# Convolution and two wide layers on one core: the two row halves of the array write the same PSUM banks by turns, without a swapped copy of x

## Chip, cores and metric

The kernel runs on one core of one Trainium2 chip, in one launch. The metric is the device time of the program in microseconds, lower is better.

## What is computed

The inputs are x (2 x 4096 tokens x 192) and weight_gen (2 x 4096 x 8 heads x 7 taps) in float32, and two pairs of weights (192 x 2048 and 2048 x 192) that arrive as float64. Cut to what matters:

```
w   = softmax(weight_gen over its 7 taps)
y   = causal convolution of x, 7 taps, one set per token and head (24 channels a head)
h1  = y @ w_in1;   y2  = max(0.01*h1, h1) @ w_out1        # layer 1
h2  = y2 @ w_in2;  out = max(h2, 0)**2 @ w_out2           # layer 2
```

## The kernel before

**Arithmetic.** TensorE works on fp32r. Every operand is split into a high part and a low remainder (xh, xl; gh, gl; wh, wl), and a product is the three terms hh, lh and hl. A float64 weight arrives as two 32-bit words; `piece` (lines 252 to 351) rebuilds a float32 from them and splits it.

**Blocks and steps.** The 8192 tokens are 16 blocks of 512. A layer takes 8 steps per block; a step makes 256 of the 2048 hidden channels with `mm1` (540 to 559) and, LAG = 2 steps later, multiplies them back to 192 with `mm2` (580 to 610). Each matmul uses 64 rows of the array: `HALVES[0]` or `HALVES[1]`, issued in pairs that run side by side. One step is 9 pairs of `mm1` and 10 of `mm2`. All matmuls of half 0 write other PSUM banks than those of half 1: in `mm1` bank d of `ph` belongs to half d, in `mm2` each half has its own accumulators pa and pb (four banks, one set, so a block's first `mm2` waits until the last block's sums are read). Because 192 input channels are 128 + 64, each half needs both halves of the first 128: `swap` (377 to 385) copies x's halves across by DMA, or `turn` (387 to 396) by TensorE for blocks 0 and 1.

**Other engines.** `activate` (561 to 578) reads `ph` twice on ScalarE in layer 1 (lines 568, 569) and takes three ScalarE operations in layer 2 (571 to 573); VectorE then makes gl (576). `local_sum` (413 to 533) computes softmax and convolution on VectorE: 7 products (473) and 6 sums (485); for block 1 five of the sums, and for most first-layer weights one sum (`plus`, 245), go through GpSimd as adding DMAs. Blocks 0 and 1 are transposed by TensorE (498), the later ones by VectorE and a trip through DRAM. `end1`/`again` (627 to 656) park layer 1's result in DRAM and bring it back; `end2` (658 to 677) adds the halves' sums, moves 64 rows by DMA, transposes and stores.

**Order.** `Plan.op` records each operation with a priority, `Plan.issue` (68 to 138) fixes the order of every engine's queue ahead of the run: an engine takes the first operation in order of priority that can start, TensorE always in strict order. The order of blocks is layer 1 of blocks 0 to 4, then layer 2 of block 0, layer 1 of block 5, layer 2 of block 1, and so on; block 1 begins at step 8.

Of the kernel before, what the change touches and what calls it, by code (L numbers as in the profile page):

```python
# [13 lines left out]
SIGN_EXP = -(1 << 23)  # L14
# [127 lines left out]
def kernel(  # L142
# [40 lines left out]
    EARLY = 2  # L183
    R = TB * H
# [19 lines left out]
    MM = 0.2345  # L204
# [14 lines left out]
    def weight_tiles(pool, l):  # L219
        wi.append({k: pool.tile([P, 3, NPR, P], F32R, name=f"wi{l}{k}") for k in "hl"})  # L220
        wo.append(pool.tile([P, NFC, 2 * D], F32R, name=f"wo{l}"))

    warm = const.tile([P, 1], F32, name="warm")
# [4 lines left out]

# [16 lines left out]
    def plus(to, tv, of, ov, pr, late):  # L245

        pl.op(
            "POOL", 1.0, pr, [of, to], [to],
            lambda: nc.gpsimd.dma_start(out=tv(), in_=ov(), accum_op=ALU.add), late=late,
        )  # L250

    def piece(kind, l, j, nj, pr, dma=False, gate=()):
# [11 lines left out]
        if kind == "i":  # L264
            src = (w_in1, w_in2)[l].rearrange("(s p) (n e m) w -> p s n e (m w)", p=Q, e=2, m=P)
            for d in range(2):

                def load(d=d):
                    to = raw.t[HALVES[d], :n, :].rearrange("p (s q m) w -> p s q (m w)", s=3, m=P)
                    for q in range(nj):  # L270
                        nc.sync.dma_start(out=to[:, :, q], in_=src[:, :, j + q, d])

                pl.op("SP", 0.5 * nj, pr - 6, [], [raw], load, late=(nj * 0.6, 3.5), after=gate[:1])
# [13 lines left out]
        def I(b):  # L287
            return b.t[:, :n].bitcast(I32)

        pl.op(  # L290
            "ACT", act(n), pr - 3, [raw], [wu, wa],
# [16 lines left out]
            "DVE", dve2(n), pr - 2, [wa], [wu],  # L308
            lambda: nc.vector.tensor_scalar(I(wu), I(wa), SIGN_EXP, None, op0=ALU.bitwise_and),  # L309
        )  # L310
        pl.op(
            "DVE", dve(n), pr - 2, [wu, raw], [wu],
            lambda: nc.vector.scalar_tensor_tensor(  # L313
                V(wu), raw.t[:, :n, 0].bitcast(U32), 2.0**-52, V(wu), op0=ALU.mult, op1=ALU.mult
            ),
        )
        if dma:
            plus(wa, lambda: V(wa), wu, lambda: V(wu), pr - 2, (nj * 0.8, 4.5))
        else:
            pl.op(  # L320
                "DVE", dve(n), pr - 2, [wu, wa], [wa],
                lambda: nc.vector.tensor_tensor(V(wa), V(wa), V(wu), op=ALU.add),
            )
        def to(hl):
            if kind == "i":
                return wi[l][hl][:, :, js, :].rearrange("p s q m -> p s (q m)")
            return wo[l][:, 2 * j : 2 * (j + nj), slice(0, D) if hl == "h" else slice(D, 2 * D)]

        def val():
            return V(wa).rearrange("p (s m) -> p s m", s=3 if kind == "i" else 2 * nj)  # L330
# [23 lines left out]
    xrows = x.rearrange("b s d -> (b s) d")  # L354
# [13 lines left out]
    XS = ("ah", "al", "sh", "sl", "bh", "bl")  # L368
# [4 lines left out]

    sets = {}
    taken = []

    def swap(xs, pr):
        for k in "hl":

            def go(k=k):  # L380
                to, of = xs["s" + k].t, xs["a" + k].t
                nc.sync.dma_start(out=to[0:Q].bitcast(F32), in_=of[Q:P].bitcast(F32))
                nc.sync.dma_start(out=to[Q:P].bitcast(F32), in_=of[0:Q].bitcast(F32))

            pl.op("SP", 1.0, pr, [xs["a" + k]], [xs["s" + k]], go, late=(0.8, 2.0))

    def turn(xs, pe, pr):

        pt = pl.buf(ps, [P, 2, N], F32, "pt", "ph", 2)
        for i, k in enumerate("hl"):  # L390
            pl.op(
                "PE", MM, pe + 0.1 * i, [xs["a" + k], perm_b], [pt],
                lambda i=i, k=k: nc.tensor.matmul(pt.t[:, i, :], lhsT=perm, rhs=xs["a" + k].t, start=True, stop=True),
            )
        for i, k in enumerate("hl"):
            pl.op("ACT", act(N), pr, [pt], [xs["s" + k]], lambda i=i, k=k: nc.scalar.copy(xs["s" + k].t, pt.t[:, i, :]))
# [16 lines left out]
    def local_sum(tb, pr, gate=()):  # L413
# [53 lines left out]

# [8 lines left out]
        for k in range(1, K):  # L476
            tmp = pl.buf(sb, [P, TB, H, G], F32, "tmp", "c", 2)
            pl.op("DVE", dve(TB * D), pr - 2, [xc, wg], [tmp], lambda k=k, tmp=tmp: prod(k, tmp.t))
            if tb == 1 and k < K - 1:
                flat = lambda: att.t[:, :, 0:D]  # L480
                plus(att, flat, tmp, lambda tmp=tmp: tmp.t.rearrange("p t h g -> p t (h g)"), pr - 2, (1.6, 4.5))
            else:
                pl.op(
                    "DVE", dve(TB * D), pr - 2, [att, tmp], [att],
                    lambda tmp=tmp: nc.vector.tensor_tensor(acc(), acc(), tmp.t, op=ALU.add),  # L485
                )
# [43 lines left out]
        if tb < EARLY:  # L530
            turn(xs, at[0, tb] - 0.3, pr - 1)
        else:
            swap(xs, pr - 1)

# [5 lines left out]
    def mm1(l, tb, j, pr):  # L540
        xs = sets[l, tb]
        ph = h_t[l, tb, j] = pl.buf(ps, [P, 2, N], F32, "ph", "ph", 2)

        def go():
            wh, wl = wi[l]["h"], wi[l]["l"]

            terms = [(w, hl, s) for ss in ("ab", "s") for w, hl in ((wh, "h"), (wl, "h"), (wh, "l")) for s in ss]
            for i, (w, hl, s) in enumerate(terms):
                for d in range(2):
                    c = 2 if s == "b" else d ^ (s == "s")  # L550
                    nc.tensor.matmul(  # L551
                        ph.t[:, d, :],
                        lhsT=w[HALVES[d], c, j, :],
                        rhs=xs[s + hl].t[HALVES[d]],
                        start=(i == 0),
                        stop=(i == len(terms) - 1),
                    )

        return pl.op("PE", 9 * MM, pr, [*xs.values(), wi_b[l][j]], [ph], go)
# [20 lines left out]
    def mm2(l, tb, j, pr):  # L580
        gh, gl = g_t.pop((l, tb, j))
        first, last = j == 0, j == NPR - 1
        if first:
            acc_t[l] = [
                [pl.buf(ps, [P, N], F32, n, f"q{2 * d + i}", 1) for i, n in enumerate(("pa", "pb"))] for d in range(2)
            ]
        acc = acc_t[l]

        def prods(terms, g, begin, end):
            for i, (c, w) in enumerate(terms):  # L590
                for d in range(2):
                    wt = wo[l][HALVES[d], 2 * j + c, :]
                    nc.tensor.matmul(  # L593
                        acc[d][w == "b"].t,
                        lhsT=wt[:, {"ah": slice(0, P), "b": slice(P, 2 * P), "al": slice(2 * P, 3 * P)}[w]],
                        rhs=g.t[HALVES[d], c, :],
                        start=begin and i == 0,
                        stop=end and i == len(terms) - 1,
                    )

        w = wo_b[l][j]
        for n, (ks, g) in enumerate(((("ah", "al"), gh), (("b",), gh), (("ah",), gl), (("b",), gl))):
            terms = [(c, k) for c in range(2) for k in ks]
            to = [a[ks[0] == "b"] for a in acc]
            pl.op(
                "PE", len(terms) * MM, pr + 0.01 * n, [g, w], to,
                lambda terms=terms, g=g, n=n: prods(terms, g, first and n < 2, last and n >= 2),
            )
        if last:
            (end1, end2)[l](tb, acc, pr - 1)  # L610


    def total(acc, i, v, hold, pr):
        o = pl.op("ACT", act(N), pr, [acc[1][i]], [v, *hold], lambda: nc.scalar.copy(v.t, acc[1][i].t))
        pl.op(
            "DVE", dve(N), pr, [acc[0][i], v], [v],
            lambda: nc.vector.tensor_tensor(v.t, acc[0][i].t, v.t, op=ALU.add),  # L617
        )
        return o

# [3 lines left out]

    kept = {}

    def end1(tb, acc, pr):
        kept[tb] = [pl.buf(dram, [P, N], F32, n, n, LEAD + 2) for n in ("ka", "kb")]
        for i in range(2):
            v, to = wide("s", ("e", 2)), kept[tb][i]  # L630
            total(acc, i, v, [], pr)
            pl.op("SP", 0.5, pr, [v], [to], lambda v=v, to=to: nc.sync.dma_start(out=to.t, in_=v.t), late=(0.8, 2.0))

    def again(tb, pr, gate):
# [9 lines left out]
        def twice():  # L644
            for v, rows in ((bu, slice(0, Q)), (bl_, slice(Q, P))):
                for d in range(2):
                    nc.sync.dma_start(out=v.t[HALVES[d]], in_=kb.t[rows])
# [121 lines left out]
```

## Time and profile before

| what | us |
|---|---|
| median of three runs | 1173.73 |
| lowest, highest run | 1172.78, 1175.06 |
| profiled execution, its span (first to last instruction) | 1175.6 |
| TensorE busy | 1125.3 (96%) |
| VectorE busy, ScalarE busy | 724.4 (62%), 748.6 (64%) |

The page has no time for the profiled execution besides its span. That lies 1.9 us above the median of the timed runs, so sums below are made against 1175.6 and their differences taken to the median. TensorE is the busy engine over most of the span; its busy time does not tell how fast it works, which has to be read from the distance of its matmuls.

### The profile page before, as it was taken

How to read it: one execution, taken by the hardware profiler on the slowest of the kernel's cores; microseconds unless marked ns; L12 is line 12 of the kernel's file. 1: busy time of each engine (PE TensorE's matmuls, PEld its weight loads, DVE VectorE, ACT ScalarE, POOL GpSimd, SP SyncE). 2: the span in 40 equal slices, each digit the busy share in tenths (PEclk: the TensorE clock that was granted, in tenths of full speed). 3: DMA queues.
4: the chain of work that ended last, by engine and by line, in shares of the span. 5: the costliest groups of instructions: out<-in, count | busy, mean ns of one | idle time of the engine just before them, and what ended most of it. 6: DMA issues, size and time to landing. Idle time of an engine off the chain costs nothing.

```text
span 1175.6 us, 22999 instructions
## 1 busy us (share of the span) xinstructions
PE 1125.3 (96%) x9748; PEld 926.9 (79%) x9748; DVE 724.4 (62%) x871; ACT 748.6 (64%) x830; POOL 15.8 (1%) x20
## 2 busy tenths in 40 slices
PE   2689999999999999999999999999999999999996
PEld 1469887888888888888888888888888888888885
DVE  7989999948556484755738475574846543344333
ACT  2545467585756748576574857657585665777774
POOL 0210000000000000000000000000000000000000
PEclk9989999999999999999999999999999999999999
DMA  8964646151421314142141513214151232121111
GB/s 183 224 108 106 143 119 169 32 146 23 120 50 60 92 41 128 19 116 53 45 107 33 136 19 100 65 34 122 27 143 19 90 80 50 48 64 37 19 20 18
DMA packets 112798, 94.29 MB, mean 80 GB/s; under 512 B 59644, under 2 KB 89114, under 8 KB 112696
## 3 DMA queue, kind: packets, MB, share of 16 engines
q1 hardware_dynamic: 108712, 87.99, 29.9%
q0 software_dynamic: 3792, 4.72, 2.5%
q8 instruction: 76, 1.25, 0.4%
q14 instruction: 26, 0.21, 0.1%
q10 hardware_dynamic: 192, 0.11, 0.0%
HBM read 50.06 MB, written 20.19 MB: 60 GB/s over the span
## 4 chain that ended last, share of the span: by engine, by line
PE 91%; DVE 6%; issue 1%; ACT 1%; DMA 1%; SPq 0%; POOL 0%; DVEq 0%; POOLq 0%; ACTq 0%
PE ph L551 43%; PE pa L593 29%; PE pb L593 19%; DVE gl L576 1%; DVE tmp L473 1%; DVE att L485 1%; DVE wa L303 0%; DVE wu L309 0%; DVE wu L313 0%; DVE wa L297 0%; DMA xc<-in_x_dram 0%; DMA wg<-in_weight_gen_dram 0%; DVE wo L345 0%; ACT g L569 0%; ACT gh L568 0%
## 5 line engine op out<-in xcount | busy, mean ns | idle before, releaser
L576 DVE TENSOR_TENSOR gl<-g,gh 128x1024 fp32r<-128x1024 f32 x256 | 312.8, 1223 | 381.1 <-ACT g L573 291.8
L568 ACT ACTIVATE gh<-ph 128x1024 fp32r<-128x1024 f32 x128 | 131.6, 1028 | 253.0 <-PE ph L551 253.0
L593 PE MATMUL pa<-gh,wo 64*128 64x512 f32 x2048 | 277.5, 389 | 3.1 <-DVE s L617 2.5
L593 PEld LDWEIGHTS pa<-gh,wo 64*128 64x128 f32 x2048 | 193.3, 185 | 47.3 <-DVE oa L617 4.1
L571 ACT ACTIVATE g<-ph 128x1024 f32<-128x1024 f32 x128 | 131.6, 1028 | 117.8 <-PE ph L551 117.8
L593 PE MATMUL pb<-gh,wo 64*128 64x512 f32 x1024 | 158.5, 387 | 0.2 <-DVE wo L345 0.2
L593 PE MATMUL pa<-gl,wo 64*128 64x512 f32 x1024 | 158.2, 386 | 0.0
L593 PE MATMUL pb<-gl,wo 64*128 64x512 f32 x1024 | 158.1, 386 | 0.0
L572 ACT ACTIVATE gh<-g 128x1024 fp32r<-128x1024 f32 x128 | 135.7, 1060 | 4.0
L573 ACT ACTIVATE g<-g 128x1024 f32<-128x1024 f32 x128 | 136.0, 1062 | 3.5
L569 ACT ACTIVATE g<-ph 128x1024 f32<-128x1024 f32 x128 | 130.5, 1019 | 0.0
L593 PEld LDWEIGHTS pb<-gh,wo 64*128 64x128 f32 x1024 | 96.9, 185 | 20.3 <-DVE wo L345 0.7
L593 PEld LDWEIGHTS pa<-gl,wo 64*128 64x128 f32 x1024 | 96.6, 184 | 19.9 <-DVE gl L576 0.4
L593 PEld LDWEIGHTS pb<-gl,wo 64*128 64x128 f32 x1024 | 96.7, 184 | 19.4
L473 DVE TENSOR_TENSOR tmp<-xc,wg 128x768 f32<-128x768 f32 x96 | 91.1, 950 | 0.0
L485 DVE TENSOR_TENSOR att<-att,tmp 128x768 f32<-128x768 f32 x91 | 86.9, 955 | 1.7
L551 PE MATMUL ph<-xah,wi0h 64*128 64x512 f32 x256 | 52.0, 400 | 7.8 <-ACT wi0h L335 7.8
L551 PE MATMUL ph<-xah,wi0l 64*128 64x512 f32 x256 | 51.9, 399 | 3.4 <-DVE wi0l L345 3.4
L551 PE MATMUL ph<-xbl,wi0h 64*128 64x512 f32 x256 | 51.5, 396 | 1.1 <-DVE xbl L408 1.1
L551 PE MATMUL ph<-xsh,wi0h 64*128 64x512 f32 x256 | 51.4, 395 | 0.0
L551 PE MATMUL ph<-xsh,wi0l 64*128 64x512 f32 x256 | 51.4, 395 | 0.0
L551 PE MATMUL ph<-xal,wi0h 64*128 64x512 f32 x256 | 51.4, 395 | 0.0
(98 smaller groups left out, 1455.0 us busy)
## 6 DMA issues: line engine op xcount, KB each, us to landing
xc<-in_x_dram SPq DMA_DIRECT2D x62, 240.0 KB, 4.5
xsh<-xah SPq DMA_DIRECT2D x60, 128.0 KB, 2.4
xsl<-xal SPq DMA_DIRECT2D x60, 128.0 KB, 2.4
raw<-in_moe_w_in_dram SPq DMA_DIRECT2D x32, 192.0 KB, 6.3
raw<-in_moe_w_out_dram SPq DMA_DIRECT2D x7, 768.0 KB, 4.7
sc<-xb SPq DMA_DIRECT2D x14, 384.0 KB, 2.4
ka<-s SPq DMA_DIRECT2D x16, 256.0 KB, 2.0
kb<-s SPq DMA_DIRECT2D x16, 256.0 KB, 3.2
```

The lines of the kernel that those rows point to most:

```text
L473: nc.vector.tensor_tensor(dst, xk, wg.t[:, :, :, k : k + 1].to_broadcast([P, TB, H, G]), op=ALU.mult)
L485: lambda tmp=tmp: nc.vector.tensor_tensor(acc(), acc(), tmp.t, op=ALU.add),
L551: nc.tensor.matmul(ph.t[:, d, :], lhsT=w[HALVES[d], c, j, :], rhs=xs[s + hl].t[HALVES[d]], start=(i == 0), stop=(i == len(terms) - 1),)
L568: pl.op("ACT", W, pr, [ph], [gh], lambda: nc.scalar.activation(gh.t, ph.t, AF.Prelu, alpha=0.01))
L569: pl.op("ACT", W, pr, [ph], [g], lambda: nc.scalar.activation(g.t, ph.t, AF.Prelu, alpha=0.01))
L571: pl.op("ACT", W, pr, [ph], [g], lambda: nc.scalar.activation(g.t, ph.t, AF.Relu))
L572: pl.op("ACT", W, pr, [g], [gh], lambda: nc.scalar.activation(gh.t, g.t, AF.Square))
L573: pl.op("ACT", W, pr, [g], [g], lambda: nc.scalar.activation(g.t, g.t, AF.Square))
L576: lambda: nc.vector.tensor_tensor(gl.t, g.t, gh.t.bitcast(F32), op=ALU.subtract),
L593: nc.tensor.matmul(acc[d][w == "b"].t, lhsT=wt[:, {"ah": slice(0, P), "b": slice(P, 2 * P), "al": slice(2 * P, 3 * P)}[w]], rhs=g.t[HALVES ...
```

## The change

- Half 0 and half 1 now add into the same banks, at different times: while half 0 writes one bank, half 1 writes another, then they change over. One `ph` bank belongs to 128 hidden channels, and there is one pa and one pb; these have a ring of four banks, two blocks' worth. No swapped x is made; `swap`, `turn` and `perm` are gone.
- A bank is handed over only after the other half's last matmul there has ended. Five times a step `word` puts a no-operation on GpSimd that waits for a matmul, and `await_` lets a later matmul wait for it. `products` orders `mm1` of step s and `mm2` of step s - 2 into one sequence of 19 pairs.
- Steps 0, 1 and the last two use all 128 rows in one matmul where they can.
- Layer 1 of blocks 0 and 1 alternates: steps 0 to 2 are block 0, then block 1 and block 0 in turn. Block 1 begins at step 3.
- A weight's low word becomes an integer on ScalarE and is added as an integer on VectorE; the exponent mask, the float multiply and the adding DMAs are gone. Input weights are loaded in longer rows.
- `end1` and `again` move 192 rows, not 256; `end2` transposes pa straight from PSUM and has no DMA between its steps. The plan's cost of a matmul, MM, is 0.2267.

In the core below, `one(d, bank, slice, w, x)` is a matmul of half d of the rows into a bank of `ph`, and `two(d, c, k, g)` one into pb where k is "b" and into pa otherwise. Within step s the groups stand in TensorE's queue as o, l1, y(gh), y(gl), w_, x_(gh), x_(gl), l2_, with 4, 2, 2, 2, 3, 2, 2 and 2 pairs. The loop over `("b",), gh` is that of the last two steps, with all 128 rows; AHEAD is 3.

```diff
+    def word(*givers):
+        n = nc.gpsimd.nop()
+        for g in givers:
+            tc.add_manual_dep(n.ins, g.ins.name, SYNC)
+        return n
...
...
+            def o():
+                for n, (k, (a, b)) in enumerate((("a", T[0]), ("b", T[0]), ("a", T[1]), ("b", T[1]))):
+                    i = [one(d, d, d if k == "a" else 2, a, k + b, start=n == 0) for d in range(2)]
+                given["p1"] = i[1]
+            def l1():
+                for c, k in enumerate("ab"):
+                    i = one(0, 0, 0 if k == "a" else 2, *("h", k + "l"))
+                    o = two(1, c, "ah", gh, start=begin and c == 0)
+                    if c == 0:
+                        await_(o, given["a"])
+                given["p"] = word(i, given["p1"])
+            def y(g, ks):
+                for n, k in enumerate(ks):
+                    i = two(0, n, "b", g, start=begin and g is gh and n == 0)
+                    if g is gh and n == 0:
+                        await_(i, given["b"])
+                    o = two(1, n, k, g)
+                if g is gl:
+                    given["ab"] = word(i, o)
+            def w_():
+                for n, (a, b) in enumerate(T):
+                    i = one(0, 1, 1, a, "a" + b)
+                    o = one(1, 0, 0, a, "a" + b, stop=n == 2)
+                    if n == 0:
+                        await_(i, given["p"])
+                        await_(o, given["p"])
+                given["p1"] = word(i)
+            def x_(g, k):
+                for n in range(2):
+                    i = two(0, n, k, g)
+                    o = two(1, n, "b", g, stop=end and g is gl and n == 1)
+                    if g is gh and n == 0:
+                        await_(i, given["ab"])
+                        await_(o, given["ab"])
+                if g is gl:
+                    given["b"] = word(o)
+            def l2_():
+                for c, k in enumerate("ab"):
+                    o = two(0, c, "ah", gh, stop=end and c == 1)
+                    i = one(1, 1, 1 if k == "a" else 2, *("h", k + "l"), stop=c == 1)
+                    if c == 0:
+                        await_(i, given["p1"])
+                given["a"] = word(o)
...
+            for n, (ks, g) in enumerate(((("b",), gh), (("b",), gl), (("ah", "al"), gh), (("ah",), gl))):
...
-            lambda: nc.vector.tensor_scalar(I(wu), I(wa), SIGN_EXP, None, op0=ALU.bitwise_and),
-                V(wu), raw.t[:, :n, 0].bitcast(U32), 2.0**-52, V(wu), op0=ALU.mult, op1=ALU.mult
-            plus(wa, lambda: V(wa), wu, lambda: V(wu), pr - 2, (nj * 0.8, 4.5))
+            lambda: nc.scalar.activation(I(wu), raw.t[:, :n, 0].bitcast(U32), AF.Copy, scale=2.0**-29),
+            lambda: nc.vector.tensor_tensor(I(wa), I(wa), I(wu), op=ALU.add),
...
+                acc_t[l2, tb2] = [pl.buf(ps, [P, N], F32, n, "acc", 4) for n in ("pa", "pb")]
...
+    steps = [(0, 0, j) for j in range(AHEAD)]
+    for j in range(NPR):
+        steps.append((0, 1, j))
+        if j + AHEAD < NPR:
+            steps.append((0, 0, j + AHEAD))
+    steps += [(l, tb, j) for l, tb in phases[2:] for j in range(NPR)]
...
+        local_sum(1, at[0, 1])
```

## Rows read from the trace of the kernel before

**Rows 1.** The page's busy times.

```profile
PE 1125.3 (96%) x9748; PEld 926.9 (79%) x9748; DVE 724.4 (62%) x871; ACT 748.6 (64%) x830; POOL 15.8 (1%) x20
```

**Rows 2.** Stretches: length, then busy us and instructions per engine, PEclk, DMA.

```profile
0.00:90.00 90.00, 52.22 (x314) 37.28 (x316) 75.72 (x116) 39.45 (x56) 15.84 (x20) 0.94 0.82 168
90.00:220.00 130.00, 126.37 (x1109) 110.53 (x1108) 120.98 (x153) 77.23 (x93) 0.00 (x0) 1.00 0.50 129
220.00:1166.80 946.80, 946.74 (x8330) 779.04 (x8326) 524.40 (x598) 631.37 (x682) 0.00 (x0) 1.00 0.26 65
```

**Rows 3.** Timeline of one layer-2 step: start, us, instruction, [idle before, releaser].

```profile
600.69 0.39 PE L551 MATMUL ph<-xah,wi1h 64*128 64x512 f32 x2
...
602.50 0.39 PE L551 MATMUL ph<-xsl,wi1h 64*128 64x512 f32 x2
602.73 1.07 PE L593 MATMUL pa<-gh,wo 64*128 64x512 f32 x8
...
602.93 1.03 ACT L571 ACTIVATE g<-ph 128x1024 f32<-128x1024 f32 x1 [1.10 <-PE ph L551]
...
605.00 0.39 PE L551 MATMUL ph<-xah,wi1h 64*128 64x512 f32 x2
```

**Rows 4.** Waits of TensorE: us in total, times, longest.

```profile
PE pt L498 <- DVE att L485: 21.7, 1, 21.7
...
PE pa L593 <- DVE s L617: 2.5, 2, 1.3
```

**Rows 5.** VectorE's groups until 215 us: count, busy us, mean ns, idle before.

```profile
L576 DVE TENSOR_TENSOR gl<-g,gh 128x1024 fp32r<-128x1024 f32 x36 | 43.6, 1218 | 5.8 <-PE pb L593 5.6
L473 DVE TENSOR_TENSOR tmp<-xc,wg 128x768 f32<-128x768 f32 x30 | 28.5, 952 | 0.0
...
L313 DVE SCALAR_TENSOR_TENSOR wu<-raw,wu 128x768 f32<-128x768 uint32 x14 | 13.4, 958 | 0.5
...
L297 DVE TENSOR_SCALAR wa<-wu 128x768 int32<-128x768 int32 x14 | 7.9, 566 | 0.7 <-ACT wu L292 0.5
```

**Rows 6.** Timeline of TensorE where block 1 begins.

```profile
84.94 0.63 PE L551 MATMUL ph<-xbh,wi0h 64*128 64x512 f32 x2
85.36 0.63 PE L551 MATMUL ph<-xah,wi0l 64*128 64x512 f32 x2
```

**Rows 7.** Timeline of TensorE around a wait in layer 1.

```profile
194.02 0.50 PE L551 MATMUL ph<-xbl,wi0h 64*128 64x512 f32 x2 [1.14 <-DVE xbl L408]
194.36 0.40 PE L551 MATMUL ph<-xsh,wi0h 64*128 64x512 f32 x2
```

**Rows 8.** Timeline and line 249: how GpSimd answers (q: its sequencer; min/median/max ns).

```profile
32.53 0.35 DVE L297 TENSOR_SCALAR wa<-wu 128x384 int32<-128x384 int32 x1
...
32.93 1.03 POOL L249 DMA_DIRECT2D wa<-wu  x1 [4.04 <-DVE wa L297]
...
L249 POOLq EVENT_SEMAPHORE  x8: 17/17/5257, 37.4 to 66.0; - x8
...
48.80 0.53 ACT L335 CAST wo<-wa 128x384 fp32r<-128x384 f32 x1
...
49.65 1.05 POOL L249 DMA_DIRECT2D wa<-wu  x1 [2.51 <-ACT wo L335]
```

**Rows 9.** Timeline of the end, TensorE's last pair of mm1 onward.

```profile
1159.56 0.39 PE L551 MATMUL ph<-xsl,wi1h 64*128 64x512 f32 x2
...
1163.23 1.23 DVE L576 TENSOR_TENSOR gl<-g,gh 128x1024 fp32r<-128x1024 f32 x1 [3.08 <-ACT g L573]
...
1166.13 0.61 PE L593 MATMUL pb<-gl,wo 64*128 64x512 f32 x4
...
1168.16 0.70 DVE L664 STREAM_TRANSPOSE ta<-oa 128x512 f32<-128x512 f32 x1
...
1168.89 2.16 SPq L669 DMA_DIRECT2D out_dram<-ta  x4
...
1172.07 0.85 SPq L669 DMA_DIRECT2D out_dram<-oa  x2
```

More of the change, by code (lines that the diff above doesn't have):

```diff
@@ L183 @@
     EARLY = 2
+    AHEAD = 3
     R = TB * H
@@ L243, in second, with piece @@
             weight_tiles(ctx.enter_context(tc.tile_pool(name="const2", bufs=1)), 1)
[L245 to L252, printed above, removed]
+    def piece(kind, l, j, nj, pr, gate=()):
         n = nj * 3 * P
@@ L264, in piece, with load @@
         if kind == "i":
[L265 to L273, printed above, removed]
+            src = (w_in1, w_in2)[l]
+            c0, c1 = 2 * P * j, 2 * P * (j + nj)
+            def load():
+                to = raw.t[:, :n, :].rearrange("p (q s m) w -> p q s (m w)", q=nj, m=P)
+                both = src[0:P, c0:c1].rearrange("p (q s m) w -> p q s (m w)", q=nj, m=P)
+                half = src[P:D, c0:c1].rearrange("p (q e m) w -> p e q (m w)", q=nj, m=P)
+                nc.sync.dma_start(
+                    out=to[:, :, 0:2].rearrange("p q s m -> p q (s m)"), in_=both.rearrange("p q s m -> p q (s m)")
+                )
+                for e in range(2):
+                    nc.sync.dma_start(out=to[HALVES[e], :, 2], in_=half[:, e])
+            pl.op("SP", 1.5, pr - 6, [], [raw], load, late=(nj * 1.2, 3.0), after=gate[:1])
         else:
@@ L375 @@
     taken = []
[L377 to L396, printed above, removed]
     def halves(xs, k, v, dep, pr, first=False):
@@ L478, in local_sum @@
             pl.op("DVE", dve(TB * D), pr - 2, [xc, wg], [tmp], lambda k=k, tmp=tmp: prod(k, tmp.t))
[L479 to L486, printed above, removed]
+            pl.op(
+                "DVE", dve(TB * D), pr - 2, [att, tmp], [att],
+                lambda tmp=tmp: nc.vector.tensor_tensor(acc(), acc(), tmp.t, op=ALU.add),
+            )
         if tb < EARLY:
@@ L538 @@
     acc_t = {}
[L540 to L559, printed above, removed]
+    SYNC = mybir.DependencyInfo(mybir.DependencyClass.Sync, mybir.DependencyReason.DATA)
@@ L578, in activate @@
         g_t[l, tb, j] = gh, gl
[L580 to L610, printed above, removed]
@@ L613, in total, with last64 @@
[L613 to L619, printed above, removed]
     def wide(name, ring=("w", 4)):
         return pl.buf(sb, [P, N], F32, name, *ring)
-    kept = {}
[L627 to L632, printed above, removed]
+    def last64(pb, v, pr):
+        pl.op("ACT", act(N), pr, [pb], [v], lambda: nc.scalar.copy(v.t[0:Q], pb.t[Q:P]))
+        pl.op(
+            "DVE", dve(N), pr, [pb, v], [v],
+            lambda: nc.vector.tensor_tensor(v.t[0:Q], pb.t[0:Q], v.t[0:Q], op=ALU.add),
+        )
@@ new lines, with end1 @@
+    kept = {}
+    def end1(tb, pa, pb, pr):
+        ka = pl.buf(dram, [P, N], F32, "ka", "ka", LEAD + 2)
+        kb = pl.buf(dram, [Q, N], F32, "kb", "kb", LEAD + 2)
+        kept[tb] = ka, kb
+        v, u = wide("s", ("e", 2)), wide("u", ("e", 2))
+        last64(pb, u, pr)
+        pl.op("ACT", act(N), pr, [pa], [v], lambda: nc.scalar.copy(v.t, pa.t))
+        pl.op("SP", 0.5, pr, [v], [ka], lambda: nc.sync.dma_start(out=ka.t, in_=v.t), late=(0.8, 2.0))
+        pl.op("SP", 0.5, pr, [u], [kb], lambda: nc.sync.dma_start(out=kb.t, in_=u.t[0:Q]), late=(0.8, 2.0))
@@ L684 @@
             phases.append((0, tb + LEAD))
-    at = {ph: i * NPR for i, ph in enumerate(phases)}
-    steps = [(l, tb, j) for l, tb in phases for j in range(NPR)]
-    one = []
+    steps = [(0, 0, j) for j in range(AHEAD)]
[4 more added lines that the diff above has]
+    steps += [(l, tb, j) for l, tb in phases[2:] for j in range(NPR)]
+    at = {ph: steps.index((*ph, 0)) for ph in phases}
+    one_ = []
     def weights(kind, l, sizes):
@@ L693, in weights @@
         for n in sizes:
-            o = piece(
-                kind, l, j, n, at[l, 0] + j + (LAG if kind == "o" else 0) - 16 * l, dma=l == 0 and j > 0, gate=one[-2:] if l else ()
-            )
+            use = steps.index((l, 0, j)) + (LAG if kind == "o" else 0)
+            o = piece(kind, l, j, n, use - 16 * l, gate=one_[-2:] if l else ())
             if l:
-                one.append(o)
+                one_.append(o)
             j += n
@@ L718 @@
         weights("o", 1, (2,) * 4)
+        local_sum(1, at[0, 1])
         starts = []
[L720 to L736 removed]
+        q = 2
+        for s in range(len(steps) + LAG):
+            if q < len(phases) and s == at[phases[q]] - NPR + LAG:
+                gate = starts[q - 2 : q - 1] if q > 2 else ()
+                lq, tq = phases[q]
+                if lq:
+                    again(tq, at[lq, tq] - 3, gate)
+                else:
+                    local_sum(tq, at[lq, tq] - 4, gate)
+                q += 1
+            before = len(pl.ops)
+            products(s)
+            if s < len(steps) and steps[s][2] == 0:
+                starts.append(pl.ops[before])
         pl.issue()
```

155 lines of the change are left out of this document (84 added, 71 removed).

## Prediction

> **What bounds the kernel now.** I read the busy times first, then the stretches, then the timeline of one step, then the waits. TensorE is busy 96% of the span [rows 1]; that says who bounds it, not how fast it goes. Its pace stands in the timeline: a layer-2 step begins at 600.69 and the next at 605.00, so 19 pairs take 4.31 us, 0.2267 us a pair [rows 3]. The 9748 matmuls [rows 1] less 16 transposes and 4 of `turn` are 4864 pairs, or 1102.7 us at this pace. The other 73 us of the span are what can be won, and the stretches say where they lie [rows 2]. Until 90 us there are 294 matmuls of the layers (314 less the 20), 147 pairs or 33.3 us of work: 56.7 us lost. From 90 to 220 some 554 pairs, 125.7 us: 4.3 us lost. From 220 to 1166.8 the 4165 pairs fill 944.3 of 946.8 us: 2.5 us lost. After the last matmul, whose group begins at 1166.13 and whose last start is one pair later, 9.2 us go by [rows 9]. So the steady part is at its pace, and the change can win at the start, a little in the middle, and at the end.
>
> The start is VectorE's: it is busy 75.7 of the first 90 us [rows 2], and TensorE's longest wait, 21.7 us, is for block 0's convolution sums [rows 4].
>
> **The change, part by part.**
>
> *Pairs.* Steps keep 19 pairs; the steps with all 128 rows take as many slots as before. `turn` (4 matmuls) goes. The pace of a pair, 0.2267, stays: both halves still write different banks at any moment. Zero.
>
> *Handovers.* Five a step, each a signal from a matmul, a no-operation on GpSimd, and a wait on TensorE. The tightest is from the end of y(gl) to x_: with w_'s 3 pairs between, the receiver is due 4 pairs after the giver's start, 0.91 us. It must be let go earlier by its weight load, which is the step from 0.23 to 0.34 us in the pair after a wait: 0.11 [rows 7]. That leaves 0.80 us. What is needed: from the start of the giving matmul to another engine's start 0.43 us (602.50 to 602.93) [rows 3]; GpSimd's sequencer 0.02 us (its semaphore instructions' median, 17 ns); back to an engine 0.05 us, as from VectorE's end at 32.88 to GpSimd's start at 32.93 [rows 8]. Sum 0.50 us, 0.30 us to spare; the other four handovers have 0.23 us more or better. GpSimd has nothing else to do, since its adding DMAs go too. I take zero, the value nearest to those rows. The far end: GpSimd's slow answers, such as 0.32 us from ScalarE's end (48.80 + 0.53) to 49.65 [rows 8], belong to DMA issue; with that the chain is 0.43 + 0.32 + 0.05 = 0.80 us and the reserve is gone. A gain is excluded, because pairs cannot be closer than now.
>
> *Later activation.* `ph` is now complete only at a step's end, not after its 9th pair, and gl is wanted after 8 pairs of the next step but one. From `ph`'s last start to the first such matmul there are 19 + 1 + 8 = 28 pairs, 6.3 us, where before there were 44, 10 us. The chain of layer 2 takes 1159.56 to 1164.46, 4.9 us [rows 9]; it fits with 1.4 us to spare, layer 1's two ScalarE operations with about 2.4. One operation of 0.95 us ahead of gl on VectorE [rows 5] is covered by that, a run of three is not. In 90 to 220 us VectorE is busy 121 of 130 us [rows 2], so I set 1.5 us of new stalls there (bounds 0 and 7) and none later, when it is busy 55%.
>
> *Two sets of accumulators.* The wait for the last block's sums (2.5 us in its two long cases [rows 4]) and its small form at later block ends go: with them 4.3 + 2.5 us of the middle can vanish. They would be replaced by the 1.5 us above. Middle: 6.8 to 1.5, minus 5.3.
>
> *Weights.* A full piece had on VectorE 0.57 + 0.96 + 0.57 + 0.96 and a sum and a difference of 0.96 each, where the sum was not GpSimd's [rows 5]; it now has 0.57 + 0.96 + 0.96 + 0.96 = 3.45 us, and one more ScalarE operation, hidden (ScalarE is busy 39 of the first 90 us [rows 2]). No row shows an integer sum of two tensors; it lies between 0.57 us (the integer shift) and twice the float row, 1.9; I take 0.96, its operand count's row. The longer load rows and the missing swaps (the DMA queues are busy 26% after 220 us [rows 2]) are hidden.
>
> *Start.* Block 1 is wanted at step 3 now, not 8, so its convolution, 7 products and 6 sums of about 0.93 us each, moves ahead on VectorE, and its five GpSimd sums come back to VectorE. Block 0 is unchanged until 21.7 us [rows 4]. After it VectorE has, by priority: four half pieces (0.6 of a full one, 2.05 each, an estimate by width) 8.2; the full piece i2 3.4; two lows of x 1.3 and block 1's softmax, six small operations, 2.1 (both estimates by width from the same rows); block 1's 13 operations 12.1. That ends at 48.8. gl of step 0 has the priority 1.2, behind block 1's products at 1.0, so it comes last: 50.0. TensorE, in strict order, stands in the middle of step 2 before y(gl) until then; its 11 remaining pairs then run 0.42 us apart, as after block 1's wait in the trace before (85.36 - 84.94), where the engine had stood still and was granted the lower of its two clock levels, 1.2 and not 2.4 GHz [rows 6], to 54.7. Then come block 1's transposes; the second needs the `ph` bank that ScalarE must first read (0.43, two reads of 1.03, and between them 0.6 for a copy of x, an estimate by width), and x is ready at about 59. By then 37 pairs are done, 8.4 us of work: 50.6 us lost, and 8 pairs more at the lower clock lose 1.6: some 52 us against 56.7. From there VectorE is ahead: per two steps (8.6 us) it owes two gl of 1.22 and one weight piece of 3.45. Minus 4.5. Bounds: gl of step 0 could fit before the products, then step 3 begins at about 52 and the loss is 45 (minus 11.5); or the integer sums take twice and the loss stays (0).
>
> *End.* After the last mm1 pair 20 slots remain, 4.5 us. The order b with gh, b with gl, then a, puts the last step's gl after 2.27 + 0.45 us of work, but gl is there only after 4.9 [rows 9]: 2.2 us of stall. After the last matmul the sums of pb are done; pa needs 0.43, a transpose of 0.70, four stores of 2.16 and a landing of 2.7 (1172.07 + 0.85 to 1175.6) [rows 9]: 6.0 in place of 9.2. Minus 1.0.
>
> **Sum.** -4.5 - 5.3 - 1.0 = -10.8 on 1175.6, and on the median of 1173.73, which lies 1.9 lower: 1163.
>
> **The rivals.**
>
> *Handovers show: slower.* If GpSimd answers as slowly as its DMA issue, or TensorE needs an extra semaphore instruction of its own for each wait, x_ comes late in each of 254 steps. It decides the sign from 10.8 / 254 = 0.043 us over the reserve, that is an answer of 0.41 us or more in place of 0.07 behind the 0.43. At 0.1 us over, 25 us: 1188. For it: GpSimd has no row of a bare no-operation. Against it: its sequencer's 17 ns, and 0.30 us of reserve. Chance 0.14.
>
> *The signals themselves cost.* Today about two matmuls a step signal; now five more do. The matmul that wakes ScalarE at 602.50 is followed by the next pair 0.23 us later like any other [rows 3], so a signal costs under the 0.01 us that the row resolves: at most 5 x 254 x 0.01 = 13 us, 1176. Chance 0.04. The Trainium skill, "TensorE: Matmul & The Clock Gate", section on the cost of the per-tile semaphore tail, gives 26.3 ns for each increment, as these are done one after another; by that an estimate of 33 us and about 1196. The trace here does not bear that out between pairs.
>
> *Activation late.* If ScalarE's copies and VectorE's other work add more than 1.4 us to the chain in part of the layer-2 steps, 0.1 us on average over 256 steps is 26 us; I price it at 0.04, 10 us, no gain: 1173. For it: the slack falls from 10 to 6.3 us. Against: ScalarE's 67% load after 220 us. Chance 0.12.
>
> *The start wins more.* gl of step 0 before block 1's products: 1156. Chance 0.13.
>
> **How the numbers follow.** Forecast 0.57. Its own range goes from 1159 (no new stalls, a little more at the start) to 1169 (the bounds 7 in the middle). For 8 in 10 I reach to 1154 and, into the slow handovers, to 1178. A difference of 0.2%, 2.3 us, is about what a measurement can tell. Faster by more: the forecast, the better start and a third of the late activation, 0.73; within: 0.09; slower: the handovers, and what is left of the others, 0.18.
>
> **What would show it.** Right: a layer-2 step at 600 us still 4.31 us; no wait of TensorE for GpSimd in the list of waits; step 3's first matmul near 59 us after a wait for block 1; no wait of pa for a sum of s; a wait of about 2 us for gl near the end, and about 6 us from the last matmul to the end. Wrong: steps of 4.4 us or more with waits for GpSimd (handovers), waits for gl all through layer 2 (activation), or step 3 before 53 us (start). If a step is 4.31 us and the time is not below 1171, my account of the start is wrong.

## Result and the profile after

The changed kernel took 1163.52 us (median; 1162.91 to 1163.83), the kernel before, timed beside it, 1174.33 (1172.78 to 1175.06): a ratio of 0.9904, with a 95% interval of 0.9891 to 0.9918. The forecast of 1163 is met. Not all of its steps are, and the traces tell them apart.

The head of the page of the changed kernel, against [rows 1]:

```profile
span 1162.0 us, 23950 instructions
...
PE 1115.8 (96%) x9712; PEld 922.0 (79%) x9712; DVE 671.5 (58%) x784; ACT 756.4 (65%) x826; POOL 1.7 (0%) x7
```

Its stretches, against [rows 2], with the same columns:

```profile
0.00:90.00 90.00, 54.17 (x389) 46.00 (x391) 78.51 (x113) 46.39 (x63) 1.70 (x7) 0.92 0.43 116
90.00:220.00 130.00, 127.56 (x1112) 105.01 (x1110) 115.68 (x143) 84.17 (x102) 0.00 (x0) 0.99 0.40 107
220.00:1154.60 934.60, 932.98 (x8214) 770.44 (x8211) 475.29 (x527) 625.43 (x663) 0.00 (x0) 1.00 0.18 44
```

The time lost is what is left of a stretch when its slots are taken at 0.2267 us. A pair of half-row matmuls is a slot, a whole-row matmul is one too (12 in steps 0 and 1, 20 in the last two), and 16 matmuls are transposes. Until 90 us: 389 - 16 - 12 = 361 halves and 12, 192.5 slots, 43.6 us of work, 46.4 lost. From 90 to 220: 556 slots, 4.0 lost. From 220 to 1154.6, with 15 of the last 20 whole-row matmuls: 4114.5 slots, 1.8 lost. Read from the last two steps alone, it is 2.1: they begin at 1148.95, and the last of their 20 slots starts at 1155.34, where 19 slots at 0.2267 us would have led to 1153.26. The table takes 2.0; such counts are good to a few tenths, since a matmul on the edge of a stretch is counted on both sides. Behind the last matmul's start, 1155.34, another 6.7 go by.

| part | before | after | difference | predicted |
|---|---|---|---|---|
| start, lost until 90 us | 56.7 | 46.4 | -10.3 | -4.5 |
| middle, lost from 90 us on | 6.8 | 4.0 | -2.8 | -5.3 |
| end: stall for the last gl, and tail | 9.2 | 2.0 + 6.7 | -0.5 | -1.0 |
| sum | | | -13.6 | -10.8 |

The spans of the two profiled executions differ by these 13.6 us (1175.6 and 1162.0), the medians by 10.8. The profiled execution of before was one of its longer ones: in every timed run the time is 1.7 to 1.9 us above its span, so this one stands for some 1177.4 us, 3.1 above the median, while over the 17 runs shown with the later experiments that kernel goes from 1172.5 to 1177.5. What makes its runs differ by 5 us stays open, and so does the part of the table in which these 3 us lie; up to 3 of the start's 10.3 may be theirs. So part of the hit is luck: in the traces the start won 5.8 us more than was said, the middle 2.5 less and the end 0.5 less, and that surplus of 2.8 is just what the base of the sum lay too high.

TensorE's waits, against [rows 4] (us in total, times, longest):

```profile
PE pt L451 <- DVE att L438: 31.4, 2, 21.6
PE pb L534 <- DVE gl L644: 4.1, 2, 2.4
PE ph L518 <- ACT wi0h L318: 1.9, 2, 1.4
PE ph L518 <- DVE wi0l L328: 1.7, 1, 1.7
PE ph L518 <- DVE xal L366: 0.6, 1, 0.6
```

No wait for GpSimd, and none of pa for the sums of the block before. The steady step, in layer 1, from its timeline (start, us, instruction):

```profile
601.91 0.39 PE L518 MATMUL ph<-xah,wi0h 64*128 64x512 f32 x2
...
603.95 0.39 PE L534 MATMUL pa<-gl,wo 64*128 64x512 f32 x1
...
604.86 0.39 PE L534 MATMUL pa<-gh,wo 64*128 64x512 f32 x1
...
606.22 0.39 PE L518 MATMUL ph<-xah,wi0h 64*128 64x512 f32 x2
```

601.91 to 606.22 is 4.31 us, as in [rows 3]. 603.95 is the last matmul of y(gl), 604.86 the first of x_ that waits for it: 0.91 us, the four pairs of the forecast, not later. GpSimd's answers, by line 493 in 600 to 606 us (minimum, median, maximum ns):

```profile
L493 POOLq EVENT_SEMAPHORE  x8: 17/17/17, 600.1 to 606.0; - x8
```

The start, from the timelines of ScalarE, VectorE and TensorE (last column: idle before, and releaser):

```profile
31.82 0.39 ACT L412 ACTIVATE wg<-wg 128x224 f32<-128x224 f32 x1
...
31.96 1.22 DVE L644 TENSOR_TENSOR gl<-g,gh 128x1024 fp32r<-128x1024 f32 x1 [1.03 <-ACT g L637]
...
36.70 0.95 DVE L430 TENSOR_TENSOR att<-xc,wg 128x768 f32<-128x768 f32 x1
...
49.44 1.94 PE L451 MATMUL pt<-ident,att 128*128 128x128 f32 x8 [9.85 <-DVE att L438]
51.95 0.79 PE L518 MATMUL ph<-xah,wi0h 64*128 64x512 f32 x2 [0.57 <-DVE xal L366]
```

The gl of step 0 ran before block 1's first product, not after its last sum. TensorE ended step 2 at 39.6 and stood for block 1 from then on; step 3 begins at 51.95, where the forecast had 59.

The middle's loss, on the same two engines:

```profile
92.51 1.18 DVE L644 TENSOR_TENSOR gl<-g,gh 128x1024 fp32r<-128x1024 f32 x1
93.74 0.50 PE L534 MATMUL pb<-gl,wo 64*128 64x512 f32 x1 [2.44 <-DVE gl L644]
...
95.99 0.62 PE L534 MATMUL pa<-gl,wo 64*128 64x512 f32 x1
...
96.42 0.62 PE L534 MATMUL pa<-gl,wo 64*128 64x512 f32 x1
```

and a stretch behind it, with the columns of [rows 2]:

```profile
95.00:98.50 3.50, 3.50 (x20) 2.71 (x20) 2.88 (x5) 0.53 (x1) 0.00 (x0) 0.53 1.04 241
```

One subtraction lay behind a solid run of block 2's products. It cost 2.44 us, and then 8 pairs 0.43 us apart, while the granted clock was 0.53, about the lower level of 1.2 GHz: another 1.6. Between the two TensorE worked on for some 1.3 us, with pairs 0.23 to 0.35 us apart.

The end, against [rows 9]:

```profile
1152.33 1.23 DVE L644 TENSOR_TENSOR gl<-g,gh 128x1024 fp32r<-128x1024 f32 x1 [3.08 <-ACT g L641]
1153.61 0.73 PE L534 MATMUL pb<-gl,wo 128*128 128x512 f32 x2 [1.62 <-DVE gl L644]
...
1155.11 0.62 PE L534 MATMUL pa<-gl,wo 128*128 128x512 f32 x2
1155.76 0.72 DVE L701 STREAM_TRANSPOSE ta<-pa 128x512 f32<-128x512 f32 x1
1156.40 0.66 DVE L699 STREAM_TRANSPOSE tu<-u 64x512 f32<-64x512 f32 x1
1156.51 1.94 SPq L696 DMA_DIRECT2D out_dram<-ta  x4
1158.55 1.00 SPq L696 DMA_DIRECT2D out_dram<-tu  x2
```

### The profile page after: what moved, and what is told of

Same layout as the page of the kernel before. It is cut to its first block, busy times and chain, and to the rows that moved or that the text cites. A ratio compares the mean times of both kernels' runs of the same rounds, so it can differ in the third digit from the quotient of the medians.

```text
span 1162.0 us, 23950 instructions
## 1 busy us (share of the span) xinstructions
PE 1115.8 (96%) x9712; PEld 922.0 (79%) x9712; DVE 671.5 (58%) x784; ACT 756.4 (65%) x826; POOL 1.7 (0%) x7
## 4 chain that ended last, share of the span: by engine, by line
PE 94%; DVE 4%; ACT 1%; DMA 0%; issue 0%; SPq 0%; POOL 0%; DVEq 0%; ACTq 0%; POOLq 0%
PE ph L518 44%; PE pa L534 30%; PE pb L534 20%; DVE att L438 1%; DVE tmp L430 1%; DVE gl L644 0%; DMA xc<-in_x_dram 0%; DVE wa L294 0%; ACT g L637 0%; DVE att L430 0%; SPq L396 0%; DVE wa L304 0%; DVE wi0l L328 0%; DVE wa L288 0%; DVEq L785 0%
## 5 line engine op out<-in xcount | busy, mean ns | idle before, releaser
L534 PE MATMUL pa<-gh,wo 64*128 64x512 f32 x2040 | 586.0, 387 | 0.0
L534 PEld LDWEIGHTS pa<-gh,wo 64*128 64x128 f32 x2040 | 376.3, 185 | 39.5
L534 PE MATMUL pb<-gl,wo 64*128 64x512 f32 x1020 | 313.6, 387 | 4.1 <-DVE gl L644 4.1
L534 PE MATMUL pb<-gh,wo 64*128 64x512 f32 x1020 | 313.5, 387 | 0.0
L534 PE MATMUL pa<-gl,wo 64*128 64x512 f32 x1020 | 313.5, 387 | 0.0
L518 PE MATMUL ph<-xal,wi0h 64*128 64x512 f32 (+1 forms) x508 | 149.3, 389 | 0.0
L518 PE MATMUL ph<-xal,wi1h 64*128 64x512 f32 x512 | 148.7, 386 | 0.0
L518 PE MATMUL ph<-xah,wi0h 64*128 64x512 f32 (+1 forms) x508 | 102.0, 392 | 2.5 <-ACT wi0h L318 1.9
L518 PE MATMUL ph<-xah,wi0l 64*128 64x512 f32 (+1 forms) x508 | 101.2, 389 | 1.9 <-DVE wi0l L328 1.7
L518 PE MATMUL ph<-xah,wi1l 64*128 64x512 f32 x512 | 99.7, 386 | 0.0
```

Of the source, the lines that this page charges most:

```text
L518: return nc.tensor.matmul(ph.t[:, bank, :], lhsT=wi[l][whl][r, j, sl, :], rhs=xs[xk].t[r], start=start, stop=stop)
L534: return nc.tensor.matmul((pb if k == "b" else pa).t, lhsT=wo[l2][r, 2 * j2 + c, COLS[k]], rhs=g.t[r, c, :], start=start, stop=stop,)
```

## Experiments

Theory at the outset: the handovers and signals are free, a step takes 4.31 us, and the gain lies in the alternation of blocks 0 and 1, in the second set of accumulators, and in VectorE's relief by the integer low word; gl is late at 91 us by its place in the order. Rivals: the alternation is the gain, or VectorE's load until about 115 us is what bounds.

**Handovers** (e5_slow1, e5_slow128, e5_slow384), three sizes of the same edit: the no-operation becomes a memset, so that GpSimd answers later by about the memset's time.

```diff
-        n = nc.gpsimd.nop()
+        n = nc.gpsimd.memset(scr[:, 0:W], 0.0)   # W = 1, 128, 384
```

> The no-operation of each handover becomes a small GpSimd memset of 128 x 1, as an answer that takes longer; all else is the changed kernel. Theory (the tightest handover has 0.30 us to spare): a memset of that size takes 0.10 us and perhaps as much again to start, so steps stay at 4.31 us and the span within 1 us of 1162.0. Rival (handovers are already at their limit): every 0.1 us shows in full, steps of 4.4 us or more, span 1187 or more.

> The same with a memset of 128 x 128, which takes 0.20 us in the kernel before. Theory: with up to 0.17 us to start it is at the edge of the 0.30 us, so 0 to 0.07 us a step, span 1162 to 1180. Rival: 0.2 to 0.4 us a step, span 1213 to 1260.

> The same with a memset of 128 x 384, some 0.35 us by the 1.05 us of 1152 columns, and up to 0.17 us to start. Theory: 0.05 to 0.25 us over the reserve at the tightest handover alone, so steps of 4.36 to 4.56 us with TensorE waiting before x_ for GpSimd, span 1175 to 1226. Rival (something else than the handover's length sets the pace, such as a slack that grows with the queue): steps stay at 4.31 us.

Measured, one run each: 1164.5, 1168.6 and 1227.0 us. The memsets of the three kernels between 600 and 800 us, by their line (minimum, median, maximum ns), one fence each:

```profile
L494 POOL MEMSET scr<- x232: 98/98/100, 600.3 to 799.4; 128x1 f32 x116
```

```profile
L494 POOL MEMSET scr<- x231: 205/205/207, 599.9 to 799.3; 128x128 f32 x116
```

```profile
L494 POOL MEMSET scr<- x219: 418/419/424, 600.3 to 799.4; 128x384 f32 x110
```

The waits of TensorE's weight loads in this slowest kernel over the same 200 us (us in total, times, longest):

```profile
PEld pa L535 <- POOL scr L494: 15.0, 44, 0.6
```

That is 44 waits, about one a step, at pa, 0.34 us each. Against the changed kernel's 1162.0 the spans are 0.7, 4.8 and 63.2 us longer, 0.00, 0.02 and 0.25 us a step over 254 steps. From 205 to 419 ns the step grows by 0.23 us, about as much as the memset (0.21): beyond the reserve the answer is paid in full, and the reserve is 0.42 - 0.25, some 0.17 to 0.19 us of memset. The forecast had 0.30 us for the no-operation. Part of the difference can be seen: in the smallest of the three the last matmul of y(gl) starts at 604.11 and the memset at 604.61, 0.50 us, where the forecast had 0.43 + 0.02. When the no-operation itself answers no row shows, so how much of the 0.30 it leaves stays open; nor does a row show the 0.17 us to start a memset that two of the expectations take. The mechanism, the place (x_) and the verdict hold. By memsets the rival's threshold is nearer than it was put: some 0.22 us of slower answer would have done, not 0.34.

**One set of accumulators, and no alternation** (e2_no_turns, e4_one_set). One set cannot hold two blocks at once, so the first of the two runs takes the alternation away, and the second the set as well.

```diff
-    AHEAD = 3
+    AHEAD = 8
 # only the second run:
-    [pl.buf(ps, [P, N], F32, n, "acc", 4) for n in ("pa", "pb")]
+    [pl.buf(ps, [P, N], F32, n, "acc", 2) for n in ("pa", "pb")]
```

> AHEAD = 8: block 1 begins at step 8, as in the kernel before; all else is the changed kernel. Theory (VectorE's work is what the start costs, and its order matters little): VectorE makes all first-layer weights, then block 1's convolution, and step 8 begins near 75 us with 132 pairs done (29.9 us of work), so 45 to 49 us are lost there against 46.4 with turns; the wait for gl near 91 us may go, so 1158 to 1165. Rival (the alternation of blocks 0 and 1 is where the start's gain of 10 us comes from): the loss at 90 us is again about 56 us, and the median 1172 or more.

> AHEAD = 8 as in the run without turns, and one set of pa and pb in place of two (the alternation needs two sets, so the two go together; to be read against that run). Theory (two sets are worth more here than the waits of the kernel before, because pa is now finished only at a step's end and wanted 5 pairs later): 0.3 to 0.6 us at each of 31 block ends, 10 to 18 us over the run without turns. Rival (only the waits of the kernel before return, 0.24 us at every second block end and a few longer ones): 3 to 7 us over it.

Measured: 1166.77 us (ratio to before 0.9930, 0.9914 to 0.9947) and 1178.77 (1.0036, 1.0026 to 1.0046). The alternation is worth 3 us, the second set 12. In the first run both the theory (1158 to 1165 us) and the rival (1172 or more) missed: until 90 us 170 slots ran, so 51.5 us are lost, 5.1 more than with turns, and from 90 to 120 us 12 slots, 2.7 us, come back (126 for 114). In the second the theory held. The late stretch of both, without the alternation first, then with one set:

```profile
220.00:1150.00 930.00, 930.00 (x8210) 768.62 (x8208) 474.32 (x527) 622.79 (x660) 0.00 (x0) 1.00 0.18 44
```

```profile
220.00:1160.00 940.00, 940.00 (x8210) 820.19 (x8210) 475.95 (x527) 622.54 (x660) 0.00 (x0) 1.00 0.18 43
```

The same 8210 matmuls need 10 us more with one set, a little under 0.4 us at each end of a block. TensorE's busy share does not fall, and under its matmuls one wait for these sums, of 0.9 us, is listed; most of the cost stands under its weight loads, here for the kernel with one set from 220 us on:

```profile
PEld pb L534 <- DVE u L656: 7.8, 26, 0.3
```

pb is free again only when VectorE has added its two halves. Before the change, with one set, all that was lost after 220 us was 2.5 us. By the order of the two kernels 13 pairs then stood between a block's last matmul into pb and the next block's first, and 8 stand there now (11 and 4 for pa). That this is why one set costs more now is argued from the order; no run varies it alone. So the second set looks less like a gain than like what this order of matmuls needs.

**The float low word, put back** (e3_float_low) on VectorE in the changed kernel, with all sums on VectorE.

```diff
-  ACT  wu = int(raw0 * 2^-29)
+  DVE  wu = wa & SIGN_EXP
+  DVE  wu = (raw0 * 2^-52) * wu
-  DVE  wa = wa + wu      (integers)
+  DVE  wa = wa + wu      (floats)
```

> The low word of the weights as before the change: exponent mask, float multiply and float sum on VectorE, no ScalarE conversion. Theory (integer sum is worth its VectorE time): 0.92 us more for each half piece and 1.53 for each full one, so block 1's first step moves from 52 to 56 or 57 us, and 12 us more VectorE work for layer 2's weights until 220 us, mostly beside TensorE: 1168 to 1172. Rival (the extra hop through ScalarE costs what VectorE saves): 1162 to 1165.

Measured: 1186.34 us (1.0096, 1.0080 to 1.0113), 22.8 us more than the changed kernel and slower than before; the theory had 5 to 9. VectorE's two added operations and the float sum until 230 us, by line, full pieces only, in this kernel (count, busy us, mean ns):

```profile
L305 DVE SCALAR_TENSOR_TENSOR wu<-raw,wu 128x768 f32<-128x768 uint32 x14 | 13.4, 958 | 0.5
...
L311 DVE TENSOR_TENSOR wa<-wa,wu 128x768 f32<-128x768 f32 x14 | 13.4, 956 | 0.4
L301 DVE TENSOR_SCALAR wu<-wa 128x768 int32<-128x768 int32 x14 | 7.8, 558 | 0.4
```

and the integer sum of the changed kernel:

```profile
L304 DVE CUSTOM_DVE_ANT_0 wa<-wa,wu 128x1536 uint16<-128x1536 uint16 x14 | 13.3, 953 | 0.4 <-ACT wu L300 0.3
```

Two stretches of the kernel with the float word:

```profile
0.00:90.00 90.00, 46.91 (x298) 36.13 (x300) 76.88 (x113) 34.37 (x47) 1.70 (x7) 0.87 0.43 116
90.00:120.00 30.00, 22.32 (x174) 19.08 (x172) 26.32 (x38) 9.66 (x11) 0.00 (x0) 0.83 0.30 69
```

Of TensorE's waits in it, that for gl, and the longest of these in the timelines of VectorE and TensorE (start, us, instruction, idle before):

```profile
PE pb L541 <- DVE gl L651: 26.6, 5, 14.4
```

```profile
53.34 1.22 DVE L651 TENSOR_TENSOR gl<-g,gh 128x1024 fp32r<-128x1024 f32 x1
...
54.62 0.79 PE L541 MATMUL pb<-gl,wo 64*128 64x512 f32 x1 [14.40 <-DVE gl L651]
```

With the half pieces (2.2 and 1.4 us) the two added operations are 24.8 us of VectorE, and the time grew by 22.8. The wait of pb for gl grew from 4.1 to 26.6 us, while that for block 1's sums, 9.8, is gone. Counted in slots, 45.5 (10.3 us) are missing until 90 us and 27 (6.1 us) between 90 and 120, where 87 ran for 114; most of the rest is missing between 160 and 300 us.

The start shows something else besides. With the float word the gl of step 0 comes at 53.34, behind all 13 operations of block 1's convolution, and TensorE stands in the middle of step 2 for 14.4 us: the order that the forecast had assumed for the changed kernel. So the edit also changed the order of VectorE's queue, which the plan fixes from its own costs, and the 22.8 us hold both. The run with AHEAD = 4 below has such a wait too (13.4 us) and loses next to nothing in all, which speaks against the order as the main price; no run has the float word with gl in its early place.

**The integer low word alone** (e9_before_int), in the kernel before. Beside the operations above, the sums of first-layer weights go from GpSimd's adding DMAs to VectorE.

```diff
-  DVE  wu = wa & SIGN_EXP;  wu = (raw0 * 2^-52) * wu
-  wa = wa + wu           (floats; VectorE or adding DMA)
+  ACT  wu = int(raw0 * 2^-29)
+  DVE  wa = wa + wu      (integers)
```

> The kernel before, with only the integer low word of the weights: mask and multiplication on VectorE go, ScalarE makes the word, and every sum is an integer sum on VectorE (the first layer's were GpSimd's adding DMAs). Theory (VectorE's relief counts where the subtraction has little slack; before it had 10 us, so here it is worth only the wait for sums in the middle and a little of the start): 1169 to 1172 us. Rival (relief of VectorE is worth the same anywhere, 23 us as in e3_float_low): 1151 us. Rival (it is worth nothing without the row halves, since TensorE's waits at the start are for block 0's convolution): 1173 to 1175 us.

Measured: 1174.23 us (1.0002, 0.9991 to 1.0012): nothing. The theory (1169 to 1172) fell, the last rival held. By VectorE's groups until 230 us the subtraction stands thus, in the kernel before and in this one:

```profile
L576 DVE TENSOR_TENSOR gl<-g,gh 128x1024 fp32r<-128x1024 f32 x40 | 48.5, 1218 | 7.0 <-PE pb L593 6.9
```

```profile
L567 DVE TENSOR_TENSOR gl<-g,gh 128x1024 fp32r<-128x1024 f32 x40 | 48.7, 1220 | 15.6 <-PE pb L584 13.9 <-ACT g L560 1.6
```

VectorE stands 13.9 us waiting for TensorE to give up an old gl, against 6.9 before; in all it is idle 36.5 us of these 230, against 23.4: the relief became idle time. The relief is smaller than in the changed kernel, because eight first-layer sums come back to VectorE: its busy time falls by 18.6 us here (724.4 to 705.8), by 25.1 there (696.6 to 671.5). It is worth nothing here and 22.8 us there. The change with the float word, all sums on VectorE, is 12 us slower than before; with the integer word it gains 10.8. This is the main finding, and no sum of parts, each priced alone, gives it. How much of the 12 us those eight sums make (6.8 us of VectorE) is not shown.

**All subtractions first, then that of step 9 alone** (e1_gl_first, e7_gl9), to take away the wait at 91 us; the second run stands on the order of the end below.

```diff
-            "DVE", dve(2 * N), pr + 0.7, [g, gh], [gl],
+            "DVE", dve(2 * N), pr + 0.7 - (3.0 if pr > 3 else 0.0), [g, gh], [gl],   # first run
+            "DVE", dve(2 * N), pr if 9 < pr < 10 else pr + 0.7, [g, gh], [gl],        # second run
```

> From step 3 on gl has a priority three steps earlier, so that block 2's convolution no longer goes ahead of it. Theory (the wait for gl near 91 us is a matter of order): that wait of 2.4 us and the 10 pairs 0.43 us apart behind it go, 4.4 us, with steps of 4.31 us from 60 us to the end: span 1157.6 in place of 1162.0, median about 1159. Rival (VectorE has no time left there): the wait comes back where block 2 begins, near 115 us, as a wait for its x, and the span stays within 1161 to 1163.

> Step 9's gl alone is put ahead of block 2's products (its key 9.5 in place of 10.2), with the last two steps in the order of e6_tail. Theory (the stall at 91 us is one subtraction that lies behind a solid run of products, and block 2's x has 1.2 us to spare): the wait of pb for gl at 91 us goes, and with it the 8 pairs at 0.427 us behind it: 2.9 + 1.6 = 4.4 us under e6_tail, about 1157.5 us. Rival (VectorE has no time to spare anywhere between 60 and 115 us, as when all subtractions were put ahead): a wait for x of block 2 or for weights takes its place behind it, and the time is 1161 to 1165 us.

Measured: 1170.23 us (0.9963, 0.9948 to 0.9978) and 1162.69 (0.9897, 0.9883 to 0.9911). The theory fell twice; of the rivals, the second run's time was right and the first's too low. Two of TensorE's waits in the first kernel, and its stretch from 90 to 120 us:

```profile
PE ph L518 <- ACT xbh L359: 2.3, 1, 2.3
PE pb L534 <- DVE wo L328: 2.3, 1, 2.3
```

```profile
90.00:120.00 30.00, 23.94 (x190) 20.37 (x188) 26.97 (x36) 13.44 (x17) 0.00 (x0) 0.90 0.31 81
```

The longest wait behind 60 us in the second kernel, and the same stretch:

```profile
PE ph L518 <- ACT xbh L359: 2.3, 1, 2.3
```

```profile
90.00:120.00 30.00, 27.27 (x224) 22.88 (x222) 28.86 (x37) 14.00 (x18) 0.00 (x0) 0.94 0.35 84
```

A wait for x of block 2 stands where that for gl was: 112 slots in the second kernel, 114 in the changed one. VectorE is busy 28.9 of these 30 us in the second kernel, and moving a wait moved it. The first kernel runs 95: a wait for weights comes on top, and the granted clock falls to 0.90.

**Block 1 one step later** (e7_gl9a4), on the second kernel above (AHEAD = 4).

> As e7_gl9, with block 1 wanted one step of block 0 later (AHEAD 4 in place of 3). Theory (3 is early enough that TensorE waits for block 1's x at 49 us, and one more step fills 4.3 us of that wait, but pushes nothing else): the loss up to 90 us falls by up to 2 us against e7_gl9. Rival (the loss is the sum of VectorE's work before 90 us, and the order of steps only moves it): the same time within 1 us as e7_gl9; with AHEAD 8 it was 3 us more.

Measured: 1163.28 us (0.9898, 0.9883 to 0.9913), the same as with 3. Its one long wait for gl, 13.4 us, takes the place of that for block 1. Until 90 us 22 slots fewer run than in the kernel with 3 (174 for 196), 5.0 us; between 90 and 120 us 19.5 more, 4.4 us. The rival is right: the order only moves the loss.

**Two taps of block 2 left out** (e10_taps; so its convolution lacks taps 5 and 6), on the order of the end below. The text on record speaks of 65 other blocks; there are 15 others.

```diff
-        for k in range(1, K):
+        for k in range(1, K - 2 if tb == 2 else K):
```

> The order of e6_tail, with the last two of the seven taps of block 2's convolution left out (two products and two sums, 3.8 us of VectorE between 90 and 110 us; 65 other blocks of the work stay whole). Theory (all of VectorE's work up to about 115 us sets the loss there, so that moving a wait only moved it and taking work away takes time away): the wait for gl at 91 us goes or is halved and no other comes in its place; 2.5 to 4.4 us under e6_tail, 1157.5 to 1159.5 us. Rival (the loss at 91 us is a matter of order alone, since gl lies behind a solid run of products, and eleven products and sums hold it up nearly as long as thirteen): 1160.5 us or more. Rival (VectorE has enough room and the loss comes from the clock after any wait): 1162 us.

Measured: 1158.04 us, 3.9 under the kernel with the same end and all taps, for 3.8 us less of VectorE. Its wait for gl, and its stretch from 90 to 120 us:

```profile
PE pb L534 <- DVE gl L644: 0.7, 1, 0.7
```

```profile
90.00:120.00 30.00, 30.00 (x268) 27.43 (x267) 27.05 (x35) 17.05 (x22) 0.00 (x0) 1.00 0.37 86
```

134 slots, full pace at full clock, and no other wait in their place. So VectorE's amount of work up to about 115 us sets TensorE's loss there: a worse order costs more, none of those tried costs less, and with 3.8 us less work the loss goes without another in its place. That it is worth 3.9 us does not price each us of VectorE's work at one: 3.9 is also the whole of that stall (4.0 with the lower clock behind it).

**Another order for the last two steps** (e6_tail): everything with gh first.

```diff
-((("b",), gh), (("b",), gl), (("ah", "al"), gh), (("ah",), gl))
+((("b",), gh), (("ah", "al"), gh), (("b",), gl), (("ah",), gl))
```

> In the last two steps pa's products with gh go ahead of pb's with gl; all else is the changed kernel. Theory (the end loses 2 us because TensorE stands before the last gl with pa's work behind it): 0.9 us of that work, four matmuls, fills the wait, so from the last gl to the last matmul's start 0.9 us less, span 1161.1. Rival (the end is set by pb's sum and its stores): the span stays at 1162.0.

Measured: 1161.97 us (0.9894, 0.9873 to 0.9914), 1.6 under the changed kernel in the medians, though the spans differ by 0.6 only. The end of its timeline:

```profile
1153.94 0.73 PE L534 MATMUL pb<-gl,wo 128*128 128x512 f32 x2 [0.68 <-DVE gl L644]
...
1155.92 1.94 SPq L696 DMA_DIRECT2D out_dram<-ta  x4
```

The stall of 1.62 us is 0.68 now. Of the 0.9 won in this stretch the spans show 0.6, because in this execution the last steps began 0.3 us later (1149.28 for 1148.95). The tail is the same 6.7. It is the fastest kernel that computes everything, by less than a measurement tells with certainty.

## Why the prediction was right, and where not

- *Handovers, signals: right.* Steps of 4.31 us, no wait for GpSimd. The reserve of 0.30 us was put too high, as far as memsets tell: 0.17 to 0.19. The Trainium skill ("TensorE: Matmul & The Clock Gate", the cost of the per-tile semaphore tail) has 26.3 ns for each increment. The traces list 2.4 signalling matmuls a step before and 6.0 after (the forecast had five more than two), and an unchanged 4.31 us does not show it.
- *Start: here a step failed, "gl of step 0 has the priority 1.2, behind block 1's products at 1.0, so it comes last: 50.0".* A priority only chooses among operations that can start. At 31.96 block 1's softmax waited for ScalarE's exponential (31.82 to 32.21), and gl ran. Step 2 ended at 39.6, and step 3 began at 51.95, not 59: the bound that the text gave as a rival (step 3 at about 52, a loss of 45; it was 46.4). The path that the step describes is there with the float word (gl at 53.34, step 3 at 62.91), and it loses 56.7 us until 90.
- *Later activation: right in place, mis-sized.* The new stall is the one between 90 and 220 us, behind a run of products, as said; there is none in layer 2. Priced at 1.5, it cost 4.0: the lower clock level after the stall, 8 pairs of 0.2 us extra, was counted in the start and left out here.
- *Two sets: right in sign.* The old waits are gone. But 12 us hang on them, not the few of [rows 4]: with the new order one set costs nearly 0.4 us a block.
- *Weights: the size of the sum was right, its worth was put into the start alone.* The sum, 0.95 us, was taken at 0.96. The run without the integer word shows 22.8 us, of which 10.3 are lost until 90 us; the run with it alone shows none. That it covers the shorter slack of gl fits both runs and is argued; no run gives gl its old slack back.
- *End: right.* Stall 2.0 us with what follows it (2.2 predicted); tail 6.7, not 6.0, since tu's two stores go out behind ta's four.

The rival "handovers show" was excluded by the runs. "Activation late" did not come where it was looked for: between 220 us and the last steps no wait for gl is listed. Without the integer low word gl is late within the first 300 us, and the time is 12 us over that of the kernel before.

## What to carry to other kernels

Where two engines lean on each other, a relief is worth what the slack of the other lets it be: price each part of a change with the slack that the other parts leave, and ask what the sum would be without it. Count the slots of work done in a stretch instead of reading busy shares; the cost at block ends stood in no busy share, and in the list of waits nearly all of what is shown (7.8 of 10 us) stands under the weight loads. Where moving a late operation only moves the wait, take work away from that engine to see whether its amount or its order bounds.

## What was not expected of the hardware

With four pairs (0.91 us) between giver and receiver, a handover from TensorE through GpSimd and back is free until GpSimd is given a memset of about 0.18 us, and what goes beyond that is paid in full every step (98 ns: 0.00, 205 ns: 0.02, 419 ns: 0.25 us a step). An integer sum of 128x768 appears in the trace as an operation on 128x1536 16-bit elements and takes 0.95 us, as the float sum does (0.956). And a single stall of 2.44 us, with 1.3 us of work behind it, was followed by 3.5 us at a granted clock of 0.53.
